# A fused attention and FFN kernel: a circular buffer for its second-level weight forms, other DMA queues, and a later place for several steps

## The chip, the cores and the metric

One core of a Trainium2 chip. The time is device microseconds (us) of one execution. The engines are called PE (TensorE, matmuls), DVE (VectorE), ACT (ScalarE), POOL (GpSimd) and SP (SyncE, which here only issues DMAs).

## The reference

```
q_n, k_n = rmsnorm(q, g_q), rmsnorm(k, g_k)          # 8 batches, 12 heads, 448 x 64, float32
scores = 1/sqrt(64) * q_n @ k_n^T
attn = exp(scores - max) / (sum + 1e-9)
x = (attn @ v) transposed to 3584 x 768              # rows are batch and position
out = square(max(x @ w_in, 0)) @ w_out               # 768 x 2048, 2048 x 768; out is 3584 x 768
```

## The kernel before

**Work.** Attention goes by pairs of heads: 8 batches x 6 pairs = 48 pairs, and the work on PE for one of them is called a visit. The FFN goes by pairs of batches, u = 0 to 3, and within each by 4 blocks of hidden columns (NBLK). A block's products are made as seven products of sums of submatrices in place of eight plain ones (PRODUCTS, L829; the sums are called forms). For u = 0 this is done at one level (`first_products`, L881, matmul L890). For u = 1 to 3 the first FFN matrix has a second level (`deep_products`, L915; `multiply`, L943, matmul L944): it needs second-level forms of the weights, 7 pieces per block (DEEP, L845), each of 10 blocks of 128 x 128 numbers that enter 11 matmuls. The second FFN matrix has one level for every u (`second_products`, L1061, matmuls L1114 and L1053).

**Stages of the trace.** 0 to 143 us: attention alone for batches 0 and 1 (`visit_alone`, L1486). 143 to 523: u = 0, with attention of batches 2 and 3 in between. 523 to 1186: u = 1 and 2, with attention of batches 4 to 7. From 1186: u = 3 alone.

**Order.** It is written out by hand. `run` (L1400) takes products from a generator until a cost is reached; after each product it issues a bit of each of several lists: a step of deep forms (`deep_to_make`), a sum of weight forms (`make_sum`, L1334), a piece of weight conversion when its time in the list `late` (L1364) has come, a step of the plan for the activations' forms (`follow_plan`, L772), attention's tasks, and up to two deferred transfers (`transfers`, L310 to L319). A visit (`visit_whole`, L1571) flushes all tasks and transfers first (`run_all`). In u = 1 and 2 a block has three visits: at 3/7 of the deep products, and after 9 and 22 products of the second matrix (`place`, L1386). `drain` (L1431) empties everything at the end of a u.

**Weights.** The weights are read as 64-bit words in 64 pieces. For each, ACT splits the words (L1227 to L1229) and DVE joins them (L1240, L1260, L1264); then first-level sums are made on DVE and POOL in turn (L1340). The conversion of block 0 is in the list `early`, that of blocks 1 to 3 in `late`. `deep_steps` (L1284) makes the second-level forms of a block: five plain copies from `in_sb` to the DRAM tensor `in_deep` (L1290, L1292), ten derived ones (`derive`, L1296, operation L1300, on DVE and POOL in turn, in four buffers `more`), each stored by L1318. Block 0's are made within the first stage, by `begin` (L1442). In u = 0 `make_all_deep` (L1326) finishes what is left after the first of a block's two groups of first products.

**Ring.** In u = 1 to 3 a piece of 10 blocks (640 KB) is read back from `in_deep` by one DMA on SP (`load_piece`, L808, DMA L816) into a ring of four pieces. A piece k is used in four parts n, in the order (k, 0), (k-1, 2), (k, 1), (k-1, 3). Piece k + 4 is loaded at step (k, 3), where piece k has been used. One pair of matmuls of each piece goes to a side bank, `aside` (L947, always bank 1). Then `put` and `put_both` empty the banks with ACT (L933, L941) or DVE (L929, L939), and the table `then` (L1000) places joins on POOL (L993) and activations on ACT (L997, L998).

**Queues.** Nearly all DMAs are issued by SP: weights, ring, q and k, v (`load_v`, L356), rows written out and read back for transposing (`store_q`, `load_blocks`), and the output rows (`store`, L1168). v goes through `transfer`, so in u = 1 and 2 it is deferred like q and k.

Of the kernel before, what the change touches and what calls it, by code (L numbers as in the profile page):

```python
# [223 lines left out]
def program(ctx, tc, rows, v, g, wide, ones, moe_w_in, moe_w_out, out, shift):  # L224
# [43 lines left out]
    arriving, transfers = deque(), deque()  # L268
# [87 lines left out]
    def load_v(i):  # L356
        b, c = pairs[i]
        values[i] = io.tile([P, NJ, 2, D], F32, name="vt", tag="vt")
        for e in range(2):
            transfer(  # L360
                values[i][:, :, e],
                rows.in_chunks(i, v[b, 2 * c + e, 0 : NJ * P]),
            )
        for odd in range(2):
            if joint(i) != (i % 2 == odd) or joint(i) and i % 2 == 0:
                h = 2 * (c - i % 2 + odd)
                transfer(
# [321 lines left out]
    def form_steps(u):  # L689
# [23 lines left out]
        def deeper(name):  # L713
# [18 lines left out]
            return [begin] + [lambda n=n: halves(n) for n in range(1, 4)]  # L732
# [17 lines left out]
        def wait(n):  # L750
            return [(0, (), None)] * n
# [7 lines left out]
        for c in range(NK):  # L759
# [4 lines left out]
            for name in (["T1", "21"], ["T2"], ["T3", "22", "T4"])[c]:  # L764
                steps += [(0, (), s) for s in deeper(name)]
        return steps

    def new_more_of_words():
        words = new_words().bitcast(F32).rearrange("p n w -> p (n w)")
        return words[:, 0 : 3 * S // 2].rearrange("p (n s) -> p n s", n=3)  # L770

# [36 lines left out]
    def load_piece(n):  # L808
# [3 lines left out]
        if n % 4 == len(ring):  # L812
            both = ffn_p.tile([P, 2, 10, P], F32, name="in_sb", tag="in_sb")
            ring.extend((both[:, 0], both[:, 1]))
        block, k = divmod(n, 7)
        nc.sync.dma_start(ring[n % 4], in_deep[block % NBLK][:, IN.index(DEEP[k][0])])  # L816
# [34 lines left out]
    def ffn(u):  # L851

        accs = [new_acc() for _ in range(2 * NT + 1)]
        for blk in range(NBLK):
# [10 lines left out]
            else:  # L865
                for t in range(2):
# [7 lines left out]
                    if t == 0:  # L874
                        make_all_deep()
                if blk == NBLK - 1:
                    for n in range(4):
                        load_piece(n)
# [36 lines left out]
    def deep_products(u, blk, hid, sums_, second):  # L915
# [31 lines left out]
        aside = banks[1][:, 0:h]  # L947

        def step(k, n):

            left, right, name, base = DEEP[k]
            if n == 0:
                ab[k] = roles[k % 3]
                w[k] = ring[(((u - 1) * NBLK + blk) * 7 + k) % 4]
# [7 lines left out]
            lhs, rhs = lambda m: w[k][:, m], x[k]  # L962
# [5 lines left out]
            elif n == 1:  # L968
                multiply(aside, lhs(1), rhs["21"], start=True)
# [3 lines left out]
                put(name, 1, a, base)  # L973
            elif n == 2:
# [5 lines left out]
            else:  # L980
                multiply(a, lhs(2), rhs["T4"])
                multiply(a, lhs(8), rhs["31"], stop=True)
                put(name, 2, a, base)
                del ab[k], w[k], x[k]
                load_piece(((u - 1) * NBLK + blk) * 7 + k + 4)
# [9 lines left out]
        def activate(name, t):  # L995
# [7 lines left out]
            (5, 2): [lambda: join("22", 0), lambda: activate("12", 0)],  # L1003
            (5, 3): [lambda: join("22", 1), lambda: activate("12", 1)],
# [56 lines left out]
    def second_products(u, blk, hid, sums_, accs):  # L1061
# [20 lines left out]
        def store_rows(tt, e):  # L1082
            queues = (nc.sync, nc.scalar if final and (tt, e) == (NT - 1, 1) else nc.sync)
# [597 lines left out]
```

## Time and profile before

| | us |
|---|---|
| median of 3 runs | 1454.86 (1454.03 to 1458.38) |
| the profiled execution, as a run | 1460.56 |
| its span in the trace | 1458.8 |
| PE busy | 1393.9 (96%) |
| POOL busy | 818.3 (56%) |
| DVE busy | 790.6 (54%) |
| ACT busy | 582.9 (40%) |

A line of a group of instructions reads: line, engine, operation, what is written <- what is read, how often, busy time. A line of a wait reads: engine and line that waited <- what ended the wait: us in total, times, the longest. In a table of stretches each engine has its busy time in the stretch, and the granted clock is a mean over it, where 1.00 is full speed. SPq is SP's queue of DMA issues; the time in its lines is that of the issue, not of the transfer. Of the chain that ended last, 71% of the span is PE, 7% DMA, 6% DVE, 4% POOL, 4% SP's queue and 3% ACT.

| DMA | times | KB each | us from issue to landing (median) |
|---|---|---|---|
| in_sb<-in_deep (pieces of the ring) | 84 | 640 | 4.8 |
| words<-in_moe_w_in_dram | 32 | 384 | 3.5 |
| words<-in_moe_w_out_dram | 32 | 384 | 3.6 |
| qk<-in_q_dram | 96 | 96 | 3.3 |
| qk<-in_k_dram | 96 | 96 | 2.6 |
| vt<-in_v_dram | 96 | 96 | 2.8 |

### The profile page before, as it was taken

The page shows a single profiled execution, that of the slowest core. Times are in us where ns is not written, and L with a number is a line of the kernel's source. Part 1 is how long each engine was busy: PE and PEld are TensorE (multiplying, and loading weights), DVE is VectorE, ACT ScalarE, POOL GpSimd, SP SyncE. Part 2 cuts the span into 40 slices and gives each one's busy share as a digit, 9 for nine tenths or more (in the row PEclk, how much of TensorE's full clock was granted, in tenths as well). Part 3 has the DMA queues.
Part 4 walks back from the last instruction along what each step waited for, and adds up shares of the span by engine and source line. Part 5 has one row for each costly group of instructions (what it writes and reads, how often), then busy time and mean ns, then how long its engine had stood idle before and what let it go on. Part 6 is the DMA issues. An engine that isn't in the chain of part 4 may idle for free.

```text
span 1458.8 us, 18023 instructions
## 1 busy us (share of the span) xinstructions
PE 1393.9 (96%) x5772; PEld 839.5 (58%) x5772; DVE 790.6 (54%) x1607; ACT 582.9 (40%) x1126; POOL 818.3 (56%) x822
## 2 busy tenths in 40 slices
PE   7988999989799999999999998999999999999998
PEld 3323444444343466575766657566674858688694
DVE  5978375686777774344445564333544555244443
ACT  6764464745546233442342433443242312221220
POOL 5657755565656687457484785755663564130312
PEclk9999999999999999999999999999999999999999
DMA  6586347667677765372746556364551626243232
GB/s 149 142 237 177 82 116 193 187 182 189 199 210 206 236 191 176 76 241 79 213 123 194 158 191 181 84 187 131 153 162 31 234 90 233 86 129 141 73 141 78
DMA packets 362221, 229.05 MB, mean 157 GB/s; under 512 B 270085, under 2 KB 339589, under 8 KB 358021
## 3 DMA queue, kind: packets, MB, share of 16 engines
q1 hardware_dynamic: 361824, 227.74, 54.1%
q8 instruction: 47, 0.77, 0.2%
q14 instruction: 58, 0.47, 0.1%
q10 hardware_dynamic: 292, 0.07, 0.0%
HBM read 172.49 MB, written 55.25 MB: 156 GB/s over the span
## 4 chain that ended last, share of the span: by engine, by line
PE 71%; DMA 7%; DVE 6%; POOL 4%; SPq 4%; issue 4%; ACT 3%; POOLq 0%; DVEq 0%; ACTq 0%
PE bank L1114 26%; PE bank L944 19%; PE bank L417 8%; PE bank L502 7%; PE bank L1053 5%; PE bank L890 4%; DMA in_deep<-more 2%; SPq L319 1%; DMA in_sb<-in_deep 1%; SPq L315 1%; DMA words<-in_moe_w_out_dram 1%; DMA q_rows<-qk 1%; POOL xT L662 1%; PE bank L528 1%; DMA out_sb<-out_forms 1%
## 5 line engine op out<-in xcount | busy, mean ns | idle before, releaser
L944 PE MATMUL bank<-xT,in_sb 128*128 128x224 f32 x1344 | 294.9, 358 | 10.3 <-DMA in_sb<-in_deep 7.2
L1167 DVE TENSOR_TENSOR acc<-acc,bank 128x384 f32<-128x384 f32 x324 | 173.8, 550 | 234.2 <-PE bank L1114 212.5
L1114 PE MATMUL bank<-out_sb,hid 128*128 128x384 f32 x768 | 270.8, 489 | 5.9 <-DVE acc L1167 3.4
L944 PEld LDWEIGHTS bank<-xT,in_sb 128*128 128x128 f32 x1344 | 256.3, 193 | 24.1 <-ACT wT L425 8.6
L425 ACT ACTIVATE wT<-bank,rr 128x448 f32<-128x448 f32 x288 | 161.3, 630 | 134.8 <-PE bank L417 121.7
L202 POOL TENSOR_TENSOR rr<-ms,minus_half 128x8 f32<-128x8 f32 (+1 forms) x96 | 145.4, 1514 | 116.7 <-DVE ms L195 108.9
L1114 PE MATMUL bank<-out_sb,sums 128*128 128x384 f32 x576 | 205.6, 489 | 3.5 <-DVE acc L1167 3.5
L1114 PEld LDWEIGHTS bank<-out_sb,hid 128*128 128x128 f32 x768 | 143.6, 190 | 112.6 <-ACT hid L998 7.9
L417 PE MATMUL bank<-qT,kT 64*128 64x448 f32 (+1 forms) x768 | 169.8, 575 | 11.4 <-ACT qT L353 10.0
L929 DVE TENSOR_TENSOR hid<-hid,bank 128x224 f32<-128x224 f32 x312 | 111.3, 383 | 115.2 <-PE bank L944 102.1
L1114 PEld LDWEIGHTS bank<-out_sb,sums 128*128 128x128 f32 x576 | 108.0, 190 | 87.1 <-DVE acc L1167 7.5
L890 PE MATMUL bank<-xT,in_sb 128*128 128x448 f32 x336 | 131.6, 545 | 0.0
L417 PEld LDWEIGHTS bank<-qT,kT 64*128 64x128 f32 (+1 forms) x768 | 57.8, 173 | 114.3 <-issue 74.5
L993 POOL TENSOR_TENSOR hid<-hid 128x448 f32<-128x448 f32 x24 | 27.2, 1140 | 170.7 <-DVE hid L929 150.4
L444 POOL TENSOR_TENSOR sum<-sum,wT 128x448 f32<-128x448 f32 (+1 forms) x96 | 113.1, 1197 | 0.8
L502 PE MATMUL bank<-wT,vt 128*64 128x448 f32 x480 | 103.4, 549 | 1.1 <-DMA vt<-in_v_dram 1.1
L997 ACT ACTIVATE hid<-hid 128x448 f32<-128x448 f32 x96 | 54.9, 572 | 119.7 <-POOL hid L993 62.6
L890 PEld LDWEIGHTS bank<-xT,in_sb 128*128 128x128 f32 x336 | 62.2, 190 | 68.6 <-issue 61.6
L1053 PE MATMUL bank<-out_sb,hid 128*128 128x384 f32 x256 | 88.3, 491 | 0.0
L944 PE MATMUL bank<-more,in_sb 128*128 128x224 f32 x288 | 76.1, 359 | 3.0 <-ACT part L941 3.0
L566 POOL COPY few<-few 32x14 f32<-32x14 f32 x48 | 9.0, 188 | 121.9 <-DVE few L564 119.8
L179 ACT ACTIVATE squares<-qk 128x512 f32<-128x512 f32 (+1 forms) x68 | 39.5, 581 | 88.5 <-DVE ms L192 46.3
(132 smaller groups left out, 1886.2 us busy)
## 6 DMA issues: line engine op xcount, KB each, us to landing
in_sb<-in_deep SPq DMA_DIRECT2D x84, 640.0 KB, 4.8
out_sb<-out_forms SPq DMA_DIRECT2D x24, 1536.0 KB, 9.7
words<-in_moe_w_in_dram SPq DMA_DIRECT2D x32, 384.0 KB, 3.5
words<-in_moe_w_out_dram SPq DMA_DIRECT2D x32, 384.0 KB, 3.6
out_forms<-out_sb SPq DMA_DIRECT2D x8, 1536.0 KB, 6.7
qk<-in_q_dram SPq DMA_DIRECT2D x96, 96.0 KB, 3.3
qk<-in_k_dram SPq DMA_DIRECT2D x96, 96.0 KB, 2.6
vt<-in_v_dram SPq DMA_DIRECT2D x96, 96.0 KB, 2.8
```

Source lines behind the costliest of these rows:

```text
L202: self.nc.gpsimd.tensor_tensor(out=self.rr[i][:, x, 0 : self.count(i)], in0=ms, in1=self.minus_half.to_broadcast(list(ms.shape)), op=ALU.pow,)
L417: nc.tensor.matmul(sc[some], lhsT=turned[p, 1][r, keys], rhs=turned[p, 0][r, :], start=True, stop=True,)
L425: nc.scalar.activation(new_weights((i, m), e), sc, AF.Exp, scale=rows.rr[i][:, 1, 2 * m + e : 2 * m + e + 1],)
L444: nc.gpsimd.tensor_tensor(out=sums[i, e][some], in0=left[some], in1=weights[key_of(i, m), e][some], op=ALU.add)
L502: nc.tensor.matmul(values_bank(i)[ds(e * D, D), :], lhsT=lasts[i % 2][mine, e, :] if m == NJ else values[i][:, m, e, :], rhs=weights[key_o ...
L890: nc.tensor.matmul(ps, lhsT=w_sb[:, IN.index(left), c, :], rhs=forms[u, c][right], start=first and c == 0, stop=c == NK - 1, skip_group_ch ...
L929: nc.vector.tensor_tensor(out=quarter(name, n), in0=quarter(base, n), in1=ps, op=ALU.add)
L944: nc.tensor.matmul(ps, lhsT=left, rhs=right, start=start, stop=stop, skip_group_check=True)
L997: nc.scalar.activation(dst, dst, AF.Relu)
L1053: nc.tensor.matmul(ps, lhsT=hid[a].rearrange("p t e s -> p t (e s)")[:, t, ds(NT * P, P)], rhs=w_sb[t][:, 2 * a + half, :], start=(a, t) = ...
L1114: nc.tensor.matmul(ps, lhsT=lefts[left][:, t, ts(tt, P)], rhs=w_sb[t][:, OUT.index(right), :], start=first and t == 0, stop=t == 1, skip_g ...
L1167: nc.vector.tensor_tensor(out=acc, in0=acc, in1=ps, op=ALU.add)
```

## The change

- The ring becomes one circular buffer of 42 blocks in two tiles of 21. The blocks of a piece are put in the order of their use (PLACES). At (k, 3) the first six blocks of piece k + 5 and the last four of piece k + 4 are loaded; where the buffer wraps, a load is split.
- v of batches 4 to 7 is loaded by ACT's queue, at the place where `load_v` stands, not deferred. The output rows of u = 0 to 2 are stored by ACT's queue too; those of u = 3 all by SP.
- In the table `then`, the two activations of "12" move from (5, 2) and (5, 3) to (5, 3) and (6, 1).
- `begin` no longer makes deep forms; `run` makes one step per product whenever there are any. All ten derived forms of a block are made by DVE. `make_all_deep` comes after both groups of first products.
- The pieces in `late` are spaced evenly, a sixteenth of a block apart, from half a block on.
- The plan for the activations' forms takes two steps per product in u = 0, makes "22" a group earlier, and leaves "T3" and "T4" beyond a mark; `drain` goes up to the mark, and the rest follows in the next pass.
- The side bank is bank 3 after a visit to an odd pair, and else bank 1.

The parts of the diff that say this:

```diff
         b, c = pairs[i]
+        queue = nc.sync if first else nc.scalar
         values[i] = io.tile([P, NJ, 2, D], F32, name="vt", tag="vt")
         for e in range(2):
-            transfer(
+            queue.dma_start(
                 values[i][:, :, e],
...
                 h = 2 * (c - i % 2 + odd)
-                transfer(
+                queue.dma_start(
                     lasts[odd][ds(odd * D, D)],
...
-            return [begin] + [lambda n=n: halves(n) for n in range(1, 4)]
+            def end():
+                halves(3)
+                whole_forms.add((u, name))
+
+            return [begin, lambda: halves(1), lambda: halves(2), end]
...
             ]
-            for name in (["T1", "21"], ["T2"], ["T3", "22", "T4"])[c]:
-                steps += [(0, (), s) for s in deeper(name)]
+            for name in (["T1", "21"], ["T2", "22"], [None, "T3", "T4"])[c]:
+                steps += [(0, (), s) for s in deeper(name)] if name else [MARK]
         return steps
...
         return words[:, 0 : 3 * S // 2].rearrange("p (n s) -> p n s", n=3)
+
+    MARK = (0, (), None)
...
-    def load_piece(n):
+    PLACES = [0, 2, 9, 1, 4, 6, 7, 3, 5, 8]
+    FIRST_PLACES, SIDE_OF_RING = 6, len(IN) * NK
+
+    def load_piece(n, second):
...
             return
-        if n % 4 == len(ring):
-            both = ffn_p.tile([P, 2, 10, P], F32, name="in_sb", tag="in_sb")
-            ring.extend((both[:, 0], both[:, 1]))
         block, k = divmod(n, 7)
-        nc.sync.dma_start(ring[n % 4], in_deep[block % NBLK][:, IN.index(DEEP[k][0])])
+        source = in_deep[block % NBLK][:, IN.index(DEEP[k][0])]
+        at, end = (FIRST_PLACES, 10) if second else (0, FIRST_PLACES)
+        while at < end:
+            side, place = divmod((n * 10 + at) % (2 * SIDE_OF_RING), SIDE_OF_RING)
+            if side == len(ring):
+                ring.append(ffn_p.tile([P, SIDE_OF_RING, P], F32, name="in_sb", tag="in_sb"))
+            size = min(end - at, SIDE_OF_RING - place)
+            nc.sync.dma_start(ring[side][:, ds(place, size)], source[:, ds(at, size)])
+            at += size
+
+    def form_of(n, m):
+        side, place = divmod((n * 10 + PLACES[m]) % (2 * SIDE_OF_RING), SIDE_OF_RING)
+        return ring[side][:, place]
...
                         yield cost
-                    if t == 0:
-                        make_all_deep()
+                make_all_deep()
                 if blk == NBLK - 1:
                     for n in range(4):
-                        load_piece(n)
+                        load_piece(n, False)
+                        load_piece(n, True)
             yield from second
...
         ab, w, x = {}, {}, {}
-        aside = banks[1][:, 0:h]
-
         def step(k, n):
...
                 ab[k] = roles[k % 3]
-                w[k] = ring[(((u - 1) * NBLK + blk) * 7 + k) % 4]
+                w[k] = ((u - 1) * NBLK + blk) * 7 + k
+                assert (u, right) in whole_forms
                 c0, c1, c2 = [forms[u, c][right] for c in range(NK)]
...
             a, b = ab[k][:, 0:h], ab[k][:, h:S]
-            lhs, rhs = lambda m: w[k][:, m], x[k]
+            lhs, rhs = lambda m: form_of(w[k], m), x[k]
             if n == 0:
...
             elif n == 1:
+                aside = banks[free_bank][:, 0:h]
                 multiply(aside, lhs(1), rhs["21"], start=True)
...
                 put(name, 1, a, base)
+                if k == 0:
+                    load_piece(w[k] + 4, False)
             elif n == 2:
...
                 put(name, 2, a, base)
+                if k < 6:
+                    load_piece(w[k] + 5, False)
+                load_piece(w[k] + 4, True)
                 del ab[k], w[k], x[k]
-                load_piece(((u - 1) * NBLK + blk) * 7 + k + 4)
                 if blk == NBLK - 1:
...
             (4, 2): [lambda: join("12", 0, "22")], (4, 3): [lambda: join("12", 1, "22")],
-            (5, 2): [lambda: join("22", 0), lambda: activate("12", 0)],
-            (5, 3): [lambda: join("22", 1), lambda: activate("12", 1)],
+            (5, 2): [lambda: join("22", 0)],
+            (5, 3): [lambda: join("22", 1), lambda: activate("12", 0)],
+            (6, 1): [lambda: activate("12", 1)],
             (6, 2): [lambda: activate("22", 0), lambda: activate("22", 1)],
...
         def store_rows(tt, e):
-            queues = (nc.sync, nc.scalar if final and (tt, e) == (NT - 1, 1) else nc.sync)
+            queue = nc.sync if final else nc.scalar
             if tt is None:
...
                 parts = [(2 * u + e, REST * e + P * tt, P)]
-            store(accs[-1 if tt is None else 2 * tt + e], parts, queues)
+            store(accs[-1 if tt is None else 2 * tt + e], parts, queue)
...
             for n, some in enumerate((upper[:, :, 0], upper[:, :, 1], lower[:, :, 1])):
-                nc.sync.dma_start(keep[:, :, n], some)
+                nc.sync.dma_start(keep[:, :, PLACES[n]], some)
             for n, some in enumerate((upper[:, :, 2], lower[:, :, 2])):
-                nc.sync.dma_start(keep[:, :, 7 + n], some)
+                nc.sync.dma_start(keep[:, :, PLACES[7 + n]], some)
...
             left, right = [x() for x in (left, right)]
-            next(sum_engines).tensor_tensor(out=made[n], in0=left, in1=right, op=op)
-            to_keep.append((keep[:, some, n], made[n]))
+            nc.vector.tensor_tensor(out=made[n], in0=left, in1=right, op=op)
+            to_keep.append((keep[:, some, PLACES[n]], made[n]))
...
     def make_all_deep():
-        while sums_to_make or forms_to_store:
+        while any(callable(some) for some in sums_to_make):
             make_sum()
...
     every = block / ahead
-    late = deque()
-    for n in range(len(all_pieces) - ahead):
-        blk, m = divmod(n, ahead)
-        late.append(blk * block + 2 + ((0.42 + 0.05 * m) * block if m < ahead // 2 else (
-            block + every * (m - ahead // 2)
-        )))
+    late = deque(
+        block + 2 + every * (n - 2 * tile_pieces) for n in range(len(all_pieces) - ahead)
+    )
...
             spent += cost
-            if deep_to_make and not sums_to_make:
+            if deep_to_make:
                 deep_to_make.popleft()()
...
             arrive()
-            follow_plan(1)
+            follow_plan(2 if first else 1)
             run_tasks(2 if cost > COST_OUT else 1)
...
         arrive(True)
-        while plan:
+        while any(some is MARK for some in plan):
             before = len(plan)
-            follow_plan(before)
+            follow_plan(1)
             assert len(plan) < before
     def begin(step):
-        if deep_to_make and not sums_to_make:
-            deep_to_make.popleft()()
         for _ in range(2):
...
     def visit_whole(i):
+        nonlocal free_bank
         run_all()
+        free_bank = 3 if i % 2 else 1
         if i <= last and not shift:
...
         for _ in ffn(B // 2 - 1):
-            pass
+            follow_plan(1)
```

More of the change, by code (lines that the diff above doesn't have):

```diff
@@ L267, in program @@
     mores, away, free, here, through_with, plan = {}, {}, {}, set(), set(), deque()
-    arriving, transfers = deque(), deque()
+    arriving, transfers, whole_forms = deque(), deque(), set()
     def whole(i):
@@ L750, in wait @@
         def wait(n):
-            return [(0, (), None)] * n
+            return [(0, (), None) for _ in range(n)]
         upper = [{(b + e, c) for e in range(2)} for c in range(NK)]
@@ L1167, in add_to, with store @@
             nc.vector.tensor_tensor(out=acc, in0=acc, in1=ps, op=ALU.add)
-    def store(acc, parts, queues):
+    def store(acc, parts, queue):
         at = 0
         for b, row, n in parts:
-            queues[at > 0].dma_start(out[ds(b * S + row, n), :], acc[at : at + n, :])
+            queue.dma_start(out[ds(b * S + row, n), :], acc[at : at + n, :])
             at += n
@@ L1378, in program @@
         nc.gpsimd.memset(ones_of[n][ds(n * LASTS, LASTS)], 1.0)
-    VISITS, last = 2, len(pairs) - 1
+    VISITS, last, free_bank = 2, len(pairs) - 1, 1
     unit = 2 * NPAIR * VISITS
```

## The prediction

> **What bounds the kernel now.** I read the page first, then the waits of TensorE (PE) stage by stage, then the issue order of the SyncE queue (SP) ahead of the late transfers.
>
> ```profile
> span 1458.8 us, 18023 instructions
> PE 1393.9 (96%) x5772; PEld 839.5 (58%) x5772; DVE 790.6 (54%) x1607; ACT 582.9 (40%) x1126; POOL 818.3 (56%) x822
> ```
>
> PE is busy for 96% of the span, and the order of its instructions stays as it is (only the side bank's number changes). So the change can win only what PE stands idle, 1458.8 - 1393.9 = 64.9 us, and what it runs at half clock. The table of stretches shows where that is (columns: PE, PE loads, DVE, ACT, POOL busy, granted clock, DMA share, GB/s):
>
> ```profile
> 14.00:143.00 129.00, 117.98 (x686) 43.20 (x688) 106.10 (x233) 86.38 (x164) 82.89 (x68) 0.96 0.69 183
> 143.00:523.00 380.00, 358.27 (x1182) 165.10 (x1174) 256.45 (x447) 195.57 (x377) 231.62 (x197) 1.00 0.64 177
> 523.00:1186.00 663.00, 646.02 (x2816) 425.36 (x2817) 303.26 (x657) 241.78 (x466) 424.92 (x464) 0.99 0.54 154
> 1186.00:1452.00 266.00, 265.83 (x1077) 202.84 (x1076) 119.38 (x257) 54.29 (x110) 72.57 (x79) 1.00 0.36 124
> 80.00:120.00 40.00, 31.58 (x172) 11.09 (x168) 30.13 (x67) 23.05 (x44) 22.50 (x20) 0.87 0.84 233
> 360.00:400.00 40.00, 32.82 (x103) 14.51 (x102) 29.95 (x46) 25.17 (x50) 28.27 (x24) 0.96 0.67 185
> 900.00:915.00 15.00, 11.49 (x43) 9.95 (x42) 4.53 (x13) 5.06 (x11) 9.01 (x9) 0.77 0.68 196
> ```
>
> Attention alone (to 143 us) leaves 11.0 us idle, the FFN with weight conversion (to 523) 21.7, the two deep FFN passes with attention (to 1186) 17.0, the last pass alone nothing (0.2). The rest is start-up and tail, which the change doesn't touch. A clock of 0.87 over 40 us is 0.13 x 40 = 5.2 us lost; so 1.6 us are lost at 360-400, 3.4 at 900-915, and in two more ten-microsecond stretches (clock 0.83) 1.7 each: 13.6 in all. The waits of PE in those stages, the first line from the first stage and the last three from the third:
>
> ```profile
> PE bank L502 <- DMA lasts<-in_v_dram: 4.3, 1, 4.3
> PE bank L417 <- ACT qT L353: 10.0, 4, 3.8
> PE bank L1114 <- DVE acc L1167: 6.9, 5, 2.8
> PE bank L545 <- ACT wT L425: 4.1, 2, 2.7
> PE bank L944 <- DMA in_sb<-in_deep: 7.2, 4, 2.8
> PE bank L944 <- ACT wT L425: 2.9, 4, 0.8
> PE bank L502 <- DMA vt<-in_v_dram: 1.1, 2, 0.7
> ```
>
> Why the transfers are late is in SP's own order. Here it is before the 2.85 us stall at 903.3-906.2:
>
> ```profile
> 886.60 0.42 SPq L816 DMA_DIRECT2D in_sb<-in_deep  x1
> 887.08 1.62 SPq L319 DMA_DIRECT2D qk<-in_k_dram  x3
> 888.80 3.91 SPq L319 DMA_DIRECT2D qk<-in_q_dram  x4
> 892.75 2.50 SPq L319 DMA_DIRECT2D qk<-in_k_dram  x4
> 895.36 2.55 SPq L319 DMA_DIRECT2D q_rows<-qk  x3
> 898.58 1.90 SPq L319 DMA_DIRECT2D qk<-q_rows  x4
> 900.53 0.48 SPq L319 DMA_DIRECT2D vt<-in_v_dram  x1
> 901.05 0.48 SPq L816 DMA_DIRECT2D in_sb<-in_deep  x1
> ```
>
> Between two pieces SP issues 19 attention transfers back to back, 14 us; the piece due at 903.3 leaves at 901.05 and lands 5.06 later (chain of waits). SP's issue time is short here, not the pieces' landing.
>
> **The Trainium skill.** (1) "TensorE: Matmul & The Clock Gate", section "HAM oscillation — how this bites in real kernels": an idle gap costs again as half clock afterwards. The trace agrees: half-clock stretches of 3.41 or 6.83 us follow the stalls of 4.33, 2.94, 3.81, 2.85 and 1.85 us. So a stall of 1.85-4.3 us is worth 1.7-3.4 us more than the wait. (2) "DMA: Bandwidth & Descriptors", section "Issuing engines are not separate DMA queues": another queue saves only the sequencer's time. The trace agrees that SP's time is what's short (14 us above). (3) "Perfetto Trace Analysis", section "Per-instruction lifecycle": activations wait in a FIFO of the engine while its sequencer goes on, but a DMA is waited for at the sequencer. The trace has four DMAs on ACT's queue, at the start only (0.22 to 0.68 us each), so it doesn't show what a waiting one holds up. (4) "SBUF — State Buffer", section "Who interferes with whom": DVE with two SBUF inputs shares a port with POOL. The trace agrees: the word join of L1264 takes 0.56 us, or 1.13 to 1.27 beside POOL.
>
> **Part by part.**
>
> *A. Deep forms of block 0 leave the first stage.* SP's five `in_deep<-in_sb` (2.68 + 3.19 = 5.9 us of issue, 74.0-80.0) stand ahead of the q, k and v loads; without them `lasts` goes at 83.3 instead of 89.2, lands 2.5 later at 85.8, and PE wants it at 87.4. That returns 4.33 us and its half clock, 3.4. Five derives leave POOL (5 x 1.15 = 5.8 us) and five leave DVE, of which one waited 4.11 us for an older store. The other stalls there (2.94, 1.30, 0.58, 0.58, 0.35 us; 1.7 half clock) wait mostly for POOL's scaling (L217, 5.2 us in 4). Everything of this: 10.1 + 5.1 = 15.2; the `lasts` stall alone: 7.7. I take **-12** (-16 to -6, as another wait may follow in this 0.84-busy DMA stretch).
>
> *B. The words evenly spaced, derives all on DVE.* Pieces of `in` now don't start before those of `out` end. The clump is at 277, 373 and 386: waits for `wT` behind the words (4.1) and 3.81 + 1.7 half clock, 9.6 in all, taken as gone. Of the 6.9 on `acc`, where DVE is 36.0 of 40 us busy (280-320), I take half, 3.4. Against it: this stage's derives on DVE go from 3 blocks x 5 to 4 x 10, so 25 more x 0.62 = +15 us on a DVE 67% busy; half falls ahead of something that PE waits for: +7. Their waits on stores (22.7 us in 6 on DVE) should fall, since one step comes per 3.4 us and four buffers give 13.6 against 3.8 to land. The 15 DMAs of block 0 (9 us of SP) go where PE doesn't stall (143-191). Net **-6** (+10 if all 15 us show and the clump merely moves; -16 if the 0.62 us all hide).
>
> *C. Circular buffer.* The four late pieces cost 7.2 and half clock 1.7 + 3.4 + 1.7, together 14.0. Pieces are 4.0 us apart when nothing disturbs (seven in 24.31 us in the last stage). The first six blocks now leave one piece earlier: those due at 903.3 would have left by 887, before the 19 transfers. The last four leave about 0.5 us sooner than 901.05 (one v transfer less), are smaller (256 KB against 640; 384 KB of words take 3.5, 96 KB of qk 2.6, so about 3.2) and land at 903.7; they are due half a piece later, 905.3. So 1.6 us of slack where there were -2.9. More loads (84 become some 196, the extra 112 x 0.43 = 48 us of SP) are paid for by 84 v loads that leave (42 us). **-12.5** (-14 to -4).
>
> *D. v and output rows on ACT's queue.* Gains: SP's v waits (1.1), **-1**. Costs: 24 visits issue 3 or 4 DMAs, 0.5 each, 1.5-2 us on ACT after the exponentials. ACT's own order at 893.3-897.1 has 3.8 us free there, so most is hidden; what stands behind are the copies of `rest` and of banks, which PE needs soon in the first block of a pass. Not shown: a DMA waiting for its buffer or for an older DMA. Bound: -1 (earlier v) to +2.2 a visit (2 us of issue and 0.2 of waiting, bare), +53. I take 0.12 a visit, **+3**. The 24 row stores follow DVE's additions, and SP waited up to 26 us for these; on ACT such a wait stops what follows, but in the last block of a pass ACT only has attention's work and `hid` behind it: 0 (to +5).
>
> *E. Side bank by parity.* After odd visits bank 1 holds the last scores and PE waits for L425 0.72 x 3 + 0.78 = 2.9; bank 3 was read one slot earlier. **-2.5** (-2.9 to 0).
>
> *F. Activations of "12" later, T3/T4 forms later.* PE's waits on `part` (3.0) come from activate("11") behind DVE, so they stay; later "12" may lengthen the wait at L1114 on L998 (1.7 in 4): 0 (-2 to +3).
>
> Sum: -12 - 6 - 12.5 - 1 + 3 - 2.5 = -31. PE then meets the next late thing: DVE and POOL remain 0.6 busy in these stages. I give a fifth back, +6: **-25**. The profiled execution took 1460.56, so 1435.6; it stands 5.7 above the median of the runs, 1454.86. From the median: 1430, taken as **1431** as the half-clock share varies.
>
> **Rivals.** *Only part returns (1443).* The DMA engines themselves limit: share 0.84 at 80-120 and 0.91 at 645-655, and in_sb landings reach 10.8 us against 4.8 typical. Then C gives 3, B nothing, A 9, E 2.5, D +3: -12. Against it: at 900-915 the share is 0.68 and lateness is issue.
> *ACT's queue becomes the bound (1477).* If each v load holds ACT's sequencer bare, 24 x 2.2 = +53 against -31: +22. It decides from 31 / 24 = 1.3 us a visit. For it: banks are emptied by ACT within few microseconds of a visit. Against: ACT is 40% busy, with 2 to 4 us free after the visits.
> *More returns (1412).* Derives hide, the DVE backlog ends (B -16), no fifth is given back: -43.
> *It doesn't do what it says:* the order of the changed program's instructions shows all parts moved, so I give this nothing.
>
> **Numbers.** Chances: forecast 0.62 (own range 1420-1442), part 0.20, ACT 0.10, more 0.08. About 0.3% (4.4 us) is what a measurement of this kernel tells from no change. A quarter of "part" is within it: faster 0.85, same 0.05, slower 0.10. The range 1410-1453 leaves out the ACT case and half of "more".
>
> **What would show it.** Right: no stall at `lasts` near 91 us and a first stage some 10 us shorter; `in_sb<-in_deep` gone from PE's waits and full clock in the deep stages; no L944 wait on L425. Wrong: PE waiting for ACT copies after visits with ACT's queue in v transfers; L417 or L1114 waiting longer on DVE in the second stage; `in_sb` still late with SP idle.

## The result, and the profile after

The changed kernel takes 1450.4 us (median of 20 runs, 1447.0 to 1452.1) beside 1455.5 for the kernel before on the same chips (20 runs, 1449.2 to 1461.7). The ratio is 0.9963 [0.9952, 0.9974]: 5 us faster, where 24 were forecast. The two profiled executions are 9.7 us apart (spans 1458.8 and 1449.1), since the one of before lies above its median.

Two parts of the forecast came, and one went the other way. Stage by stage, cut at the first matmul of each stage in the two traces (143.9 and 529.5 us before, 136.9 and 535.1 after; the first stage has the start-up in it and the last the tail):

| stage | before | forecast | after | PE idle + half-clock loss, before | the same, after |
|---|---|---|---|---|---|
| attention alone | 143.9 | -12 | 136.9 (-7.0) | 19.8 + 4.0 | 13.4 + 3.0 |
| u = 0 with words | 385.6 | -6 | 398.2 (+12.6) | 21.7 + 1.6 | 25.9 + 9.3 |
| u = 1 to 3 | 929.3 | -13 | 914.0 (-15.3) | 23.3 + 6.4 | 15.0 + 0 |

The half-clock loss is half of the time that PE worked at a granted clock of 0.5. Half clock that falls into a stall costs nothing more and isn't counted. Counted so, the two columns explain the stages: what is left of each stage's length is the same before and after within 0.7 us.

The page of the changed kernel begins:

```profile
span 1449.1 us, 18279 instructions
PE 1394.8 (96%) x5772; PEld 838.0 (58%) x5772; DVE 796.5 (55%) x1627; ACT 584.0 (40%) x1126; POOL 800.9 (55%) x802
```

The table of stretches by stage (columns as before: engines, granted clock, DMA share, GB/s):

```profile
14.00:136.00 122.00, 117.09 (x686) 43.77 (x688) 101.52 (x228) 86.02 (x164) 77.38 (x63) 0.97 0.60 156
137.00:535.00 398.00, 372.08 (x1203) 170.19 (x1200) 277.59 (x484) 197.51 (x381) 231.76 (x195) 0.97 0.67 187
535.00:1200.00 665.00, 656.18 (x2865) 432.76 (x2864) 308.94 (x675) 241.11 (x463) 423.56 (x469) 1.00 0.53 154
```

The third stage has full clock now. The second, which had it before (1.00), has 0.97. What PE waits for, the first three lines in the second stage, the next three in the third, the last in the first:

```profile
PE bank L546 <- ACT wT L426: 18.1, 4, 5.9
PE bank L1138 <- DVE acc L1191: 4.3, 4, 2.0
PE bank L418 <- ACT qT L353: 2.5, 1, 2.5
...
PE bank L963 <- ACT hid L960: 3.0, 2, 1.8
PE bank L1138 <- ACT hid L1021: 2.0, 6, 0.6
PE bank L963 <- ACT part L960: 1.9, 3, 0.7
...
PE bank L503 <- DMA lasts<-in_v_dram: 2.5, 1, 2.5
```

`in_sb<-in_deep` and the side bank's wait for the exponentials are gone, as forecast. In u = 0 the four waits for `qT` (10.0) became one (2.5), those on `acc` fell, but the wait of the denominators (L546) for the exponentials grew from 4.1 to 18.1. Three of the four are 4.7 to 5.9 us long (before 273.20, 373.46 and 474.85 us), and 6.83 us of half clock stands at each. The clock falls within the stall, so 1.3 to 2.5 us of each 6.83 pass while PE stands still, and the three together cost 7.6 us beyond the idle time. At the first of them (the two stretches are the end of the stall and what follows; the clock is the third number from the end):

```profile
271.95:273.20 1.25, 0.00 (x1) 0.04 (x1) 1.25 (x3) 1.25 (x4) 0.14 (x1) 0.50 0.00 0
273.20:278.78 5.58, 5.58 (x9) 2.14 (x10) 3.21 (x8) 3.57 (x8) 2.16 (x2) 0.50 0.77 206
```

That agrees with the Trainium skill, "TensorE: Matmul & The Clock Gate", section "HAM oscillation — how this bites in real kernels", which tells of waits of 3 to 5 us after which matmuls start throttled. The chain ahead of the same stall:

```profile
263.74 0.61 SPq L315
...
264.46 3.80 DMA words<-in_moe_w_out_dram
...
268.34 0.54 ACT words L1251
268.88 0.44 ACT words L1252
...
270.86 2.20 ACT wT L426 x4
...
273.20 1.76 PE bank L546 x4
```

SP loads a piece of words late, ACT splits it as soon as it is there, the exponentials stand behind that split, and PE stands still until they are done. The section on e1 shows how much of this stall is a loss.

### The profile page after: what moved, and what is told of

It is laid out like the page before. It is cut to its first block, busy times and chain, and to the rows that moved or that the text cites. A ratio compares the mean times of both kernels' runs of the same rounds, so it can differ in the third digit from the quotient of the medians.

```text
span 1449.1 us, 18279 instructions
## 1 busy us (share of the span) xinstructions
PE 1394.8 (96%) x5772; PEld 838.0 (58%) x5772; DVE 796.5 (55%) x1627; ACT 584.0 (40%) x1126; POOL 800.9 (55%) x802
## 4 chain that ended last, share of the span: by engine, by line
PE 79%; POOL 4%; ACT 4%; DMA 3%; SPq 3%; DVE 3%; issue 3%; ACTq 0%; DVEq 0%; POOLq 0%
PE bank L1138 28%; PE bank L963 20%; PE bank L418 9%; PE bank L503 8%; PE bank L909 5%; PE bank L1077 4%; SPq L315 1%; DMA words<-in_moe_w_out_dram 1%; PE bank L529 1%; POOL sum L445 1%; POOL sums L1063 1%; PE bank L546 1%; ACT hid L1021 1%; PE bank L515 1%; ACT wT L426 1%
## 5 line engine op out<-in xcount | busy, mean ns | idle before, releaser
L963 PE MATMUL bank<-xT,in_sb 128*128 128x224 f32 x1344 | 288.6, 354 | 0.2
L963 PEld LDWEIGHTS bank<-xT,in_sb 128*128 128x128 f32 x1344 | 252.7, 190 | 11.3 <-issue 4.3
L909 PE MATMUL bank<-xT,in_sb 128*128 128x448 f32 x336 | 136.9, 562 | 0.2 <-DVE hid L1047 0.2
```

Of the source, the lines that this page charges most:

```text
L909: nc.tensor.matmul(ps, lhsT=w_sb[:, IN.index(left), c, :], rhs=forms[u, c][right], start=first and c == 0, stop=c == NK - 1, skip_group_ch ...
L963: nc.tensor.matmul(ps, lhsT=left, rhs=right, start=start, stop=stop, skip_group_check=True)
```

## The experiments

Each stands beside the kernel before, on one chip in each group. The kernel before had medians of 1456.1 to 1458.7 in these groups, so the ratios say more than differences of medians across groups.

| kernel | us | ratio to before |
|---|---|---|
| the change | 1450.4 | 0.9963 [0.9952, 0.9974] |
| e1 old times of the pieces | 1441.3 | 0.9884 [0.9861, 0.9908] |
| e2 derives in turn | 1450.7 | 0.9949 [0.9932, 0.9967] |
| e4 v and rows on SP | 1449.2 | 0.9938 [0.9915, 0.9961] |
| e5 u = 0 as before | 1447.5 | 0.9928 [0.9906, 0.9951] |
| e6 pieces 0.035 apart | 1445.0 | 0.9918 [0.9897, 0.9939] |
| e7 e6, deep forms later | 1448.8 | 0.9947 [0.9926, 0.9968] |
| e8 copies one per step | 1448.7 | 0.9951 [0.9935, 0.9967] |
| e9 e1, rows on SP | 1442.5 | 0.9913 [0.9891, 0.9934] |
| e10 before with the buffer alone | 1445.9 | 0.9917 [0.9892, 0.9943] |
| e11 no deep forms, blocks 1-3 | 1426.0 | 0.9775 [0.9750, 0.9801] |
| e12 e1, v and rows on SP | 1440.2 | 0.9873 [0.9846, 0.9900] |
| e13 e1, copies one per step | 1442.2 | 0.9894 [0.9866, 0.9922] |
| e14 derived, not stored | 1429.5 | 0.9804 [0.9781, 0.9826] |
| e15 stored, not derived | 1447.9 | 0.9935 [0.9915, 0.9955] |
| e16 split later | 1450.5 | 0.9956 [0.9941, 0.9972] |
| e17 e12, split later | 1440.4 | 0.9886 [0.9861, 0.9911] |
| e18 e12, deep DMAs on ACT | 1434.3 | 0.9859 [0.9829, 0.9889] |
| e19 e12, deep DMAs on POOL | 1445.4 | 0.9922 [0.9893, 0.9951] |

### Which part of the change costs in u = 0: e1, e2, e5

e1, against the changed kernel:

```diff
-    late = deque(
-        block + 2 + every * (n - 2 * tile_pieces) for n in range(len(all_pieces) - ahead)
-    )
+    late = deque()
+    for n in range(len(all_pieces) - ahead):
+        blk, m = divmod(n, ahead)
+        late.append(blk * block + 2 + ((0.42 + 0.05 * m) * block if m < ahead // 2 else (
+            block + every * (m - ahead // 2)
+        )))
```

> The changed kernel with the times of the weight pieces (the list late) as they were before; all else changed. Theory W: in u = 0 the exponentials stand on ACT behind the split of words that SP loads late, behind attention's transfers and the five plain copies of the deep forms, and PE reaches that place earlier than before; the spacing is not the cause. W: 1447 to 1454, the waits of PE for the exponentials at the denominators (18.1 us in the changed kernel) stay above 10. Rival L (the even spacing costs what u = 0 lost, 12 us): 1436 to 1441, these waits back to about 4.

1441.3, at the upper edge of rival L's range, so theory W falls: the even spacing costs 9 us by the medians. The two formulas give the same times for the pieces of the second matrix; only those of the first matrix differ (0.42 to 0.77 of a block before, 0.5 to 0.94 now). The waits at L546 are 6.9 us (rival L said about 4), and half clock costs 6.7 where it cost 9.3. u = 0 is 391.5 us long, 6.7 less.

PE runs its matmuls in the same order in all these kernels, so they can be lined up. Here is the matmul at the end of the first long stall, in the kernel before, in the change and in e1:

```profile
277.15 0.97 PE L545 MATMUL bank<-sum,ones 128*64 128x448 f32 x4 [1.36 <-ACT wT L425]
273.20 1.76 PE L546 MATMUL bank<-sum,ones 128*64 128x448 f32 x4 [5.92 <-ACT wT L426]
273.37 0.97 PE L546 MATMUL bank<-sum,ones 128*64 128x448 f32 x4 [1.06 <-ACT wT L426]
```

In e1 it starts at the same time. e1 has lost the same 5 us before, in shorter waits and some half clock, and so comes later to this place. This stall itself is no loss beside e1, as W had said; the half clock at it is (2.3 us). The second long stall costs 1.6 us beside e1 and the third all of its 5.3, and half clock on top (0.7 and 2.3). The words tell the same. Those of the first stall leave at 264.46 in the change; in e1 they leave as late (first line). Those of the third leave 5.4 us later in the change (second line) than in e1 (third line):

```profile
264.54 0.42 SPq L1237 DMA_DIRECT2D words<-in_moe_w_out_dram  x1
466.30 0.53 SPq L1237 DMA_DIRECT2D words<-in_moe_w_out_dram  x1
460.94 0.42 SPq L1237 DMA_DIRECT2D words<-in_moe_w_out_dram  x1
```

e2:

```diff
-            nc.vector.tensor_tensor(out=made[n], in0=left, in1=right, op=op)
+            next(sum_engines).tensor_tensor(out=made[n], in0=left, in1=right, op=op)
```

> The changed kernel with the derived forms made by DVE and POOL in turn again. Theory W: 1448 to 1453, since the split waits for SP's transfer and not for DVE. Rival D (all derives on DVE block the word joins, and so free the words' buffers late): 1438 to 1444, and the waits for the exponentials at the denominators fall below 8 us.

1450.7, the waits 16.4. The derives on DVE cost nothing that shows.

e5 is e1 and e2 together, and (the loop of `make_all_deep` is as before, too):

```diff
     def begin(step):
+        if deep_to_make and not sums_to_make:
+            deep_to_make.popleft()()
...
-            if deep_to_make:
+            if deep_to_make and not sums_to_make:
...
-                make_all_deep()
+                    if t == 0:
+                        make_all_deep()
```

> The changed kernel with all that concerns the weight conversion and deep forms of u = 0 undone: old times of the pieces, derives in turn, block 0's deep forms in the first stage, finished after the first group. Kept: the buffer, the ACT queue, the side bank, the plan, the later activations. Theory: deep stages keep their 15 us, the first stage loses its 7, u = 0 is back at about 386: 1440 to 1444. If u = 0's loss comes from something else: 1450 to 1457.

1447.5, neither of the two; 6 us more than e1. In the traces the first stage is 145.3 us beside e1's 136.2, u = 0 387.4 beside 391.5. So taking block 0's deep forms out of the first stage returns 9 there in this pair; by the medians 6 remain, so some 3 are paid again in u = 0. One place shows it: in the change, and in the 14 experiments that keep these forms in u = 0 on SP's queue, PE waits 1.3 to 3.1 us for exponentials near 177 us. Before, and in e5 and e10, where they are made in the first stage, there is no such wait.

### The deep stages and ACT's queue: e10, e4, e9, e12

e10, against the kernel before (`load_piece`, `form_of` and PLACES as in the change):

```diff
-                w[k] = ring[(((u - 1) * NBLK + blk) * 7 + k) % 4]
+                w[k] = ((u - 1) * NBLK + blk) * 7 + k
...
-            lhs, rhs = lambda m: w[k][:, m], x[k]
+            lhs, rhs = lambda m: form_of(w[k], m), x[k]
...
+                if k == 0:
+                    load_piece(w[k] + 4, False)
...
+                if k < 6:
+                    load_piece(w[k] + 5, False)
+                load_piece(w[k] + 4, True)
...
-                load_piece(((u - 1) * NBLK + blk) * 7 + k + 4)
```

> The kernel before with the circular buffer alone (42 blocks, first six and last four, blocks in order of use); nothing else changed. If the buffer carries the gain of the deep stages as forecast (12.5 of the 15.3 us that they fell by): 1442 to 1445 beside 1456, waits for in_sb under 1 us, the waits for the side bank stay at 2.9. If it needs v off SP's queue, or if the gain came from the later plan and the side bank: 1448 to 1452.

1445.9, 0.9 us above the range of the first case and clear of the other: the buffer alone is faster than the whole change, by 11.3 us against the kernel before in the same group. In its trace the deep stages take 913.7 us (929.3 before) and u = 0, where hardly anything differs from before, 388.6 (385.6), with no wait for `in_sb` left, while the waits that other parts aim at stay:

```profile
PE bank L957 <- ACT wT L425: 2.9, 4, 0.8
PE bank L957 <- ACT part L954: 2.8, 4, 0.8
PE bank L1131 <- ACT hid L1015: 1.7, 4, 0.7
```

e4 (e9 is e1 with the last pair of these lines alone, e12 is e1 and e4 together):

```diff
-        queue = nc.sync if first else nc.scalar
...
-            queue.dma_start(
+            transfer(
                 values[i][:, :, e],
...
-                queue.dma_start(
+                transfer(
                     lasts[odd][ds(odd * D, D)],
...
-            queue = nc.sync if final else nc.scalar
+            queue = nc.sync
```

> The changed kernel with v and the output rows back on SP's queue, deferred as before. If the circular buffer alone carries the gain of the deep stages: 1449 to 1453, with the waits for in_sb at most 1 us and for vt about 1. If the ACT queue costs as forecast (3 us): 1447. If the buffer needs SP's relief: 1456 to 1460, in_sb late again by several us.

> The changed kernel with the old times of the pieces (1441.3 alone) and with the output rows on SP's queue; v stays on ACT's queue. In the changed kernel PE waits 1.26 and 1.75 us for ACT's copies of hid where a pass begins, against 0.36 and 0.45 with all on SP, so the rows on ACT should cost 2 us: 1438.5 to 1440. If v is what costs: 1441 as before.

> The changed kernel with the old times of the pieces, and v and rows all on SP's queue. The rows alone on SP left the waits of 1.29 and 1.13 us where a pass begins, so v on ACT should be what costs there: 1439 to 1440.5, these waits back to 0.4. If ACT's queue costs nothing: 1441 to 1442.

e4 took 1449.2: the buffer needs no relief of SP. e9 took 1442.5, a miss: the rows cost nothing, and PE's waits for ACT's copies at the beginning of a pass stayed (1.29 and 1.13 us). In e12 (1440.2) they are down to the last line here, and the deep stages are 2 us shorter (911.3 beside e1's 913.3; e4 has 911.8 beside the change's 914.0):

```profile
PE bank L962 <- ACT part L959: 2.6, 4, 0.7
PE bank L1137 <- ACT hid L1020: 2.2, 7, 0.6
PE bank L962 <- DVE hid L947: 0.8, 1, 0.8
PE bank L962 <- ACT hid L959: 0.4, 1, 0.4
```

So v on ACT's queue costs 2 us by the traces. By the medians (1441.3 and 1440.2, intervals overlapping) it can't be told from nothing.

### Where the deep forms stand: e6, e7, e8, e13

The list of even spacing ends at 0.94 of the block, and a block's deep forms begin when its last piece is joined. Before, SP issued block 1's five plain copies at 229.8 to 235.3; now it does so at 245.9 to 253.2, right ahead of a visit's loads. SP's order in the changed kernel:

```profile
245.49 0.35 SPq L1237 DMA_DIRECT2D words<-in_moe_w_out_dram  x1
245.93 2.83 SPq L1314 DMA_DIRECT2D in_deep<-in_sb  x3
248.81 4.34 SPq L1316 DMA_DIRECT2D in_deep<-in_sb  x2
253.25 2.55 SPq L315 DMA_DIRECT2D q_rows<-qk  x3
257.54 1.89 SPq L315 DMA_DIRECT2D qk<-q_rows  x4
259.48 2.40 SPq L315 DMA_DIRECT2D qk<-in_q_dram  x4
261.92 2.43 SPq L315 DMA_DIRECT2D qk<-in_k_dram  x4
264.46 0.53 SPq L1237 DMA_DIRECT2D words<-in_moe_w_out_dram  x1
```

e6, against e1, and then what e7 adds:

```diff
-        late.append(blk * block + 2 + ((0.42 + 0.05 * m) * block if m < ahead // 2 else (
+        late.append(blk * block + 2 + ((0.5 + 0.035 * m) * block if m < ahead // 2 else (
...
-            if deep_to_make:
+            if deep_to_make and cost == COST_IN:
```

> The changed kernel with the pieces of the first matrix from half a block on, as in the change, but 0.035 of a block apart, so that they end at 0.75 of the block and not at 0.94. Theory P (place): with even spacing the deep forms (five plain copies that hold SP 7 us, ten stores) fall into the first half of the next block, where SP has to feed the words and the visit's loads, so words come late, the exponentials stand behind the split on ACT, and PE's stall gets long enough for half clock. P: 1441 to 1445, waits for the exponentials at the denominators below 9 us. Rival N (what matters is that no such piece comes before half a block, since they lie beside the accumulations): 1449 to 1453, as the changed kernel.

> As the kernel with the pieces 0.035 of a block apart, and the deep forms' steps are held back to the first products of the next block; word pieces at the same times. P: 1448 to 1453, the waits at the denominators are back above 12 us with half clock behind them. If the place of the deep forms doesn't matter: the same as that kernel.

1445.0 and 1448.8, both within what P said, and the waits at L546 are 7.4 and 13.1. Yet the pair doesn't prove P: in the two profiled executions u = 0 has the same length (396.2 both): e6 waits longer for `qT` (4.1 against 1.2) and for ACT's `part` (1.6, against none), and loses 1.5 us more to half clock. They differ by 3.4 in the first stage, where the programs are alike, mostly by half clock there. The runs of the two don't overlap (1441.8 to 1445.2, and 1446.5 to 1450.8), so the 3.9 us are there, but the traces don't show where they come from. The place decides which wait comes; that it decides the sum is not shown. That e6 is slower than e1 goes with its pieces lying wholly beside the accumulations (it waits 8.1 for DVE's `acc`, e1 5.3); other causes weren't tried.

e8 (`raws` holds the five copies, and `raw` issues one of them); e13 is e1 with the same:

```diff
         def both(make):
+            if raws:
+                raw()
             if len(to_keep) > 1 or not make:
```

> The changed kernel with the five plain copies of a block's deep forms issued one per step, each beside a derived form, not all in one step. If it is the 7 us of SP's issue in one go that makes words late: 1442 to 1446, the waits at the denominators below 10 us. If it is the sum of all SP work in that half block, or DVE's wait for the stores of derived forms: 1448 to 1453.

> The changed kernel with the old times of the pieces and the five plain copies one per step. With even spacing that took 11 us off the waits at the denominators, but most of it came back in waits for DVE. If the stage has a common limit (DVE behind stores and words), the same here: 1440 to 1443. If the two add up: 1437 to 1439.

1448.7 and 1442.2: nothing gained. In e8 the first wait fell from 18.1 to 6.8, and others rose by as much:

```profile
PE bank L1138 <- DVE acc L1191: 9.3, 3, 5.8
PE bank L546 <- ACT wT L426: 6.8, 4, 2.8
PE bank L418 <- ACT qT L353: 5.6, 1, 5.6
```

### What of the deep forms costs: e11, e14, e15

In all three `load_piece` reads `in_deep[0]`. Then e11, e14 and e15 in turn:

```diff
-            some = deep_steps(t // 2, in_sb[t - 1], dst)
+            some = deep_steps(0, in_sb[t - 1], dst) if t == 1 else []
```

```diff
         def both(make):
+            if blk:
+                if make:
+                    make()
+                return
...
-        return [raw] + [lambda make=make: both(make) for make in steps + [None, None]]
+        return [raw][blk > 0 :] + [lambda make=make: both(make) for make in steps + [None, None]]
```

```diff
+            if blk:
+                made[n] = upper[:, some, n % NK]
+                to_keep.append((keep[:, some, PLACES[n]], made[n]))
+                return
             left, right = [x() for x in (left, right)]
```

> The changed kernel without the deep forms of blocks 1 to 3: they are neither made nor stored, and all blocks of u = 1 to 3 read block 0's, so the work left out is 15 copies and 30 derived forms within u = 0. Theory P: the deep forms' place is what loads u = 0; without them 1432 to 1438, waits at the denominators below 5 us and at most two half-clock stretches in the stage. Rival: words and attention alone make ACT late: 1445 to 1450.

> The changed kernel where the deep forms of blocks 1 to 3 are derived by DVE (30 operations) but neither they nor the 15 plain copies go to DRAM; all blocks of u = 1 to 3 read block 0's. If SP's queue and the DMAs make the words late: close to the kernel without these deep forms (1426), 1426 to 1431. If DVE's time (18.6 us and its waits) does: 1442 to 1449.

> The changed kernel where the forms of blocks 1 to 3 are stored (30 stores and the 15 copies, from the weights as they are) but not derived, so the stored values are not the forms and DVE has 30 operations less; all blocks read block 0's. If SP's queue and the DMAs make the words late: 1445 to 1449. If DVE's time and its waits for stores do: 1427 to 1433.

1426.0, below the range of either theory, 1429.5 and 1447.9, both as the first case said. Without the deep forms u = 0 takes 374.1 us, 24 less. DVE's 30 operations alone bring 3.5 back, the DMAs alone 22. That is what these DMAs cost with even spacing; what they cost with the old times, where they are issued as well, wasn't run. e15 has the same wait as the change:

```profile
PE bank L546 <- ACT wT L426: 17.9, 4, 5.8
```

Without deep forms (e11) SP's order at the place shown above is:

```profile
247.50 0.35 SPq L1237 DMA_DIRECT2D words<-in_moe_w_out_dram  x1
247.94 1.58 SPq L315 DMA_DIRECT2D q_rows<-qk  x3
252.15 1.89 SPq L315 DMA_DIRECT2D qk<-q_rows  x4
254.09 2.40 SPq L315 DMA_DIRECT2D qk<-in_q_dram  x4
256.53 2.43 SPq L315 DMA_DIRECT2D qk<-in_k_dram  x4
259.06 0.53 SPq L1237 DMA_DIRECT2D words<-in_moe_w_out_dram  x1
```

The words leave at 259.06 and not at 264.46, although the piece ahead of them left 2 us later: between the two pieces SP needs 11.6 us and not 19.0, and the five copies take 7.2. But e1, which has no copies there, sends these words at 264.54, so the copies are not the only thing that can hold them.

### Can ACT's order or another queue mend it: e16, e17, e18, e19

e16 (`end_split` splits the piece in `to_split`; `run` calls it for the next product); e17 is e12 with that. Below it e18, in which the three DMA lines of `deep_steps` change so; e19 has `nc.gpsimd` there:

```diff
-            split_words(n)
+            to_split.append(n)
...
             make_sum()
+            end_split()
             end_join()
```

```diff
-                nc.sync.dma_start(*to_keep.popleft())
+                nc.scalar.dma_start(*to_keep.popleft())
```

> The changed kernel with ACT's split of a piece of words issued one product later; loads and joins stay where they are. If the exponentials' standing behind a split that waits for late words is what PE waits for: the waits at the denominators fall from 18.1 us to below 9, 1442 to 1446. If the visit only meets the next late thing (as with the copies apart): 1448 to 1452.

> Old times of the pieces, v and rows on SP's queue (1440.2 together), and the split one product later. If the later split takes half of the 6.3 us at the denominators and what follows at half clock: 1435 to 1438; if other waits take its place: 1439 to 1441.

> Old times of the pieces, v and rows on SP's queue (1440.2 together), and the deep forms' 15 DMAs a block on ACT's queue. If SP's queue being held is the cause: 1430 to 1437, less than the 20 us that leaving them out would give, as ACT now issues them ahead of exponentials. If it is their traffic: 1439 to 1442. If ACT held by them is worse than SP: above 1443.

> The same with the deep forms' DMAs on POOL's queue. If SP's queue being held is the cause: 1428 to 1435. If it is their traffic: 1439 to 1442. If POOL, held at its queue by waits for DVE, then makes sums late: above 1442.

e16 took 1450.5 and e17 1440.4: no gain, as the rival said, though in e16 the wait at L546 fell to 12.7. e18 took 1434.3, the best of those that leave nothing out; u = 0 is 384.7 us (393.9 in e12), and its waits are:

```profile
PE bank L417 <- ACT qT L353: 6.9, 4, 3.9
PE bank L1137 <- DVE acc L1190: 5.3, 5, 2.8
...
PE bank L545 <- ACT wT L425: 2.0, 2, 1.3
```

The traffic is the same, so part of the 22 us seems to be the time in which these DMAs hold SP's queue: 6 by the medians. It is not clear of noise: e12 stood on another chip, and the intervals of the two ratios overlap. Five traces with the old times and the DMAs on SP (e1, e9, e12, e13, e17) have 388.6 to 393.9 for u = 0. e19, on the same chip as e18, took 1445.4, and there the intervals are apart. With it goes that POOL takes longer for each issue; that this is the cause wasn't tested.

```profile
L1341 POOL DMA_DIRECT2D in_deep<-more x40: 752/770/1630, 152.9 to 466.9; - x40
L1313 POOL DMA_DIRECT2D in_deep<-in_sb x12: 928/1017/1212, 149.0 to 428.9; - x12
L1315 POOL DMA_DIRECT2D in_deep<-in_sb x8: 1376/1495/1614, 151.5 to 430.4; - x8
```

These are ns, shortest, median and longest: 53 us of POOL in all, where spans on POOL are rough. On ACT's queue the medians are 367, 584 and 765.

## Why the prediction was wrong, point by point

**B, the words: the step that failed.** Forecast -6, measured +12.6 in the traces. It said "Pieces of `in` now don't start before those of `out` end", which is so, and put the 9.6 us of waits and half clock behind the words as "taken as gone". The even spacing didn't remove them: the wait at the denominators went from 4.1 to 18.1, and going back to the old times returns 9 us by the medians (e1). What the forecast didn't ask is where the pieces end and what their end sets off: the deep forms, whose five copies and ten stores moved from the end of one block into the first half of the next, among the words and a visit's loads. That this move is what makes the even spacing cost is argued: it fits the third long stall and not the first (e1), and e6 and e7 don't settle it.

By the traces the 12.6 are: even spacing 6.7 (398.2 - 391.5, e1), block 0's deep forms 4.1 (391.5 - 387.4, e5), and 1.8 that e5 still has over before. Only the first is clear: e1, e9 and e12, which differ in u = 0 only by the queue of its output rows, have 391.5, 388.6 and 393.9.

Inside the step other terms were wrong too. Block 0's DMAs, "9 us of SP", were put "where PE doesn't stall (143-191)", and there a new wait of 2.1 us stands (177.55). The other three blocks' DMAs were taken as not moved. DVE's waits on stores "should fall" from 22.7 us and rose to 33.7. The +7 for DVE was nothing (e2) or some 3.5 for all its derives in blocks 1 to 3 (e14).

**Half clock.** u = 0's idle time grew by 4.2 us only; 7.7 more were lost at half clock. The forecast priced half clock as something that goes with stalls that go. It didn't price that a few longer stalls in the place of many short ones bring it. Its rule that "a stall of 1.85-4.3 us is worth 1.7-3.4 us more than the wait" is too simple: in the same trace stalls of 2.81 us (299.36), 2.72 (373.54) and 2.25 (452.38) brought none. And it added half clock that lies within a stall: of the 6.83 us at the stall of 4.33, 2.3 pass in the stall itself, so that stall was worth 6.6 us and not 7.7.

**A.** Forecast -12, measured -7.0 in the trace; 17 traces with this first stage have 133.3 to 136.9 us, their median 135.5, which is -8.4. The stall at 91.7 went as worked out. Another came at 108.88, for the same `lasts`, 2.5 us and half clock: SP had eight q and k loads ahead of it, 7 us. "Another wait may follow" stood there and gave the size of the range, but the next visit's SP order, which was in the trace, wasn't read. Some 3 us of the gain are paid again in u = 0 (e5).

**C.** Right: forecast -12.5, and the buffer alone brings -15.6 in the deep stages of its trace and -11.3 by the medians (e10). SP's 19 transfers between two pieces are 18 in the lines shown, which changes nothing.

**D.** +3 - 1 was near to what the traces show, +2, at another place: at the beginning of a pass, and by v, not by the rows (e9, e12). That it came out near is partly luck, as the visits, for which it was worked out, show no such cost.

**E, F.** The side bank's 2.9 is gone from the waits. One new wait for DVE came, 0.79 us at 883; which of the later parts brings it wasn't separated. `part` still waits 1.9.

**The rivals.** None was the case. "Only part returns" came nearest in time (1443), but by a mechanism that isn't there: the DMA engines' share wasn't what kept the gains small, since the buffer gave all of its own. The ACT rival's 2.2 us a visit was 2 us in all. The sum of "More returns" doesn't come out: B at -16 in place of -6 gives -41, not -43.

**What stays open.** Why even spacing costs 9 us: the place of the deep forms is the likely cause, but e6 and e7 leave it open, and the first long stall has late words without it. And how much of the 22 us is SP's time and how much the traffic: e18 points to 6, not clear of noise, and ACT pays for the issue there.

## What to carry to other kernels

When a step's due times are stretched, ask what its last piece sets off and where that lands; count the DMAs of the follower in the queue's order, as with any moved step. Line up the same matmul in two traces before a stall is called a loss: the stall of 5.9 us was none beside e1, which had waited as long in smaller parts. Here waits that were taken out came back elsewhere (e8, e16), and where short waits merged into one of 5 us, half clock was added to it. Try a change of many parts one part at a time: the buffer alone (0.9917) was better than all parts together (0.9963).

## What the runs showed of the hardware

The issue of a DMA isn't always small beside its transfer. The five plain copies at 245.93 held SP 0.6 to 2.8 us each, 7.2 in all, and landed 4.3 to 6.7 us after their issue began. The Trainium skill, "DMA: Bandwidth & Descriptors", section "Issuing engines are not separate DMA queues", calls the issue usually small; here the measurement decides. The copies and stores of the deep forms issue in medians of 0.37, 0.58 and 0.77 us on ACT's queue (e18), 0.49, 0.66 and 1.45 on SP's (the change), and 0.77, 1.02 and 1.50 on POOL's (e19).

Half clock comes in stretches of 3.41 or 6.83 us in all these traces, but for the last one of each span. The length of a stall alone doesn't tell whether it comes: a wait of 2.1 us near 177 us brought it in e12 and none in the change.
